# Softmax sums beside the next batch's projections, and loads that wait for the spread of the inverses

## The chip, the cores and the metric

The kernel runs on one core of a Trainium2 chip. The metric is the device time of one execution in microseconds. An engine here is TensorE (PE, matrix products into PSUM), VectorE (DVE), ScalarE (ACT), GpSimd (POOL, which here only starts the loads) or SyncE (SP, which starts stores, on-chip copies and transposes by DMA). Each engine works through its own queue in order and waits on semaphores of the others.

## The reference

Linformer attention is followed by a feed-forward layer with squared ReLU. There are 8 batches, 8 heads, 1024 tokens and 64 channels a head; keys and values are projected from 1024 tokens down to 64.

```
k_proj = einsum('ks,bhsd->bhkd', E, k)           # E, F: 64 x 1024
v_proj = einsum('ks,bhsd->bhkd', F, v)
scores = q @ k_proj^T / sqrt(64)
attn   = exp(scores - max) / (sum(exp(scores - max)) + 1e-9)
x      = attn @ v_proj          # then heads side by side: 8192 x 512
h      = maximum(x @ w_in, 0)   # w_in: 512 x 2048
out    = (h * h) @ w_out        # w_out: 2048 x 512
```

Inputs and output are float32; the kernel multiplies in bf16 and sums in float32 in PSUM.

## The kernel before, in words

**Tiling.** A batch's 1024 tokens form two chunks of 512. The two products of the feed-forward layer are done per chunk by a scheme with seven half-size products in place of eight: operands are first added and subtracted on VectorE (`x_sum`, `w_in_sum`, `s12`, `w_out_sum`), and TensorE then multiplies 128x128 weights by 256 columns. The first product goes by groups of four 128-column blocks of w_in (class `Group`, seven products `p1` to `p7` into four PSUM banks named `ps_bank`, L669); the second goes by `second_spread` into two banks named `ps_second` (L583).

**Steps.** TensorE's order is written out by hand; the other engines' orders come from a scheduler. In the steady part (`both()`) one step is four matmuls of a first product of one chunk, then four of a second product of the chunk before. 28 steps make a chunk and 56 a batch. `at(step, ...)` and `on(step, batch, name)` put a stage of the attention behind a given step. For the loop variable b these steps count from t = 56(b-1)+28; at t+1 the feed-forward work has reached the second chunk of batch b, and the attention of batch b+1 is being finished while that of batch b+2 is begun.

**Attention stages of a batch.** Heads go by pairs, `pr` = 0 to 3.
- `project` (L270, L271): K times E into rows 0 to 63 (`LO`) of the first bank of `ps_att`, V times F into rows 64 to 127 (`HI`) of the second bank; `ps_att` is one buffer of two banks. The other half of each bank is not written. `keep_k` copies K's projection twice into `kp` on VectorE, `keep_v` copies V's into `vp` once on ScalarE and once on VectorE.
- `transpose_k_dma` and `transpose_q_dma` (SP): DMA transposes kp to kT and Q_sb to qT. qT, kT and Q_sb have one buffer each.
- `scores` (L339): two 512-column matmuls into ps_att, then the exponential on ScalarE into `expT`.
- `sums_spread(pr)` (L392): the sums of the exponentials of pairs pr and pr+1, by eight matmuls of 32 columns of ones, into all of ps_att: each pair and each head of it has 32 equal rows of its own. ScalarE takes the logarithm and exp(-x) of 128x1024, which is the inverse (`inv`), and SP copies it by eight DMAs of 32 rows into the two `rs` tiles that the values need (L403). The tag `rs` has three buffers.
- `values(pr)` (L415): four matmuls into ps_att; VectorE multiplies by rs into xT (L419).

The eight quarters of work in sums and values follow this table, whose entries are output rows, bank, head in the pair and input rows:

```
VALUE_QUADS = ((LO, 0, 0, LO), (HI, 1, 1, HI), (HI, 0, 1, LO), (LO, 1, 0, HI))
```

**Loads.** POOL starts them with conversion to bf16: 1 MB of bf16 each for K_sb, V_sb and Q_sb of a batch (L89), one buffer each. In the steady part load_q of batch b+2 is placed at t+11 and waits for the multiplication by rs of pair 1 of batch b+1 (`done`); load_kv of batch b+3 is placed at t+32 and waits for the transpose of K of batch b+2 (`kT_done`). Stores (`put`, L577, 256 KB each, three buffers `o_sb`) stand in SP's queue among the transposes and spreads: four a chunk.

Of the kernel before, what the change touches and what calls it, by code (L numbers as in the profile page):

```python
# [1 line left out]

# [7 lines left out]
P = 128  # L10
F32 = mybir.dt.float32
BF16 = mybir.dt.bfloat16
AF = mybir.ActivationFunctionType
ALU = mybir.AluOpType
PE = mybir.EngineType.PE
LO, HI = slice(0, 64), slice(64, 128)
# [3 lines left out]
def kernel(  # L20
# [11 lines left out]
    nc = tc.nc  # L32

    B, H, S, D = q.shape
# [10 lines left out]
    TCH = S // 2  # L45
# [10 lines left out]
    const_pool = ctx.enter_context(tc.tile_pool(name="const", bufs=1))  # L56
# [4 lines left out]
    soft_pool = ctx.enter_context(tc.tile_pool(name="soft", bufs=3))  # L61
# [5 lines left out]
    turn = {"att": 0, "bank": 0, "step": 1, "pairs": 2}  # L67
# [7 lines left out]
    def att_psum(shape=(P, 2, TCH), dtype=F32):  # L75
        turn["att"] += 1
        return pair_psum(turn["att"] % turn["pairs"], shape, dtype)
# [34 lines left out]
    for g in range(2):  # L112
        h = slice(2 if g == 0 else 4, 4 * g + 4)
# [8 lines left out]
    zeros = const_pool.tile([P, 512], BF16, name="zeros")  # L122
    nc.vector.memset(zeros[:], 0.0)
    ones = const_pool.tile([P, D], BF16, name="ones")
# [7 lines left out]
    for j, (lo, hi) in enumerate(W_IN_PIECES):  # L132
        t = wpool.tile([P, NCB, (hi - lo) * P], BF16, name=f"w_in_{lo}")
# [7 lines left out]
    for j in range(WP):  # L141
        t = wpool.tile([P, fn, DM], BF16, name=f"w_out_{j}")
# [10 lines left out]
    def tt(o, x, op, y):  # L153
        return nc.vector.tensor_tensor(out=o, in0=x, in1=y, op=op)  # L154
# [72 lines left out]
    for h in half:  # L227
        nc.scalar.copy(kp[:, h].rearrange("p h a d -> p (h a d)"), zeros[:])
    kT = const_pool.tile([P, H, 2, KP], BF16, name="kT")
    VALUE_QUADS = ((LO, 0, 0, LO), (HI, 1, 1, HI), (HI, 0, 1, LO), (LO, 1, 0, HI))  # L230

    class Attention:
# [30 lines left out]
            nc.scalar.copy(self.vp[HI], view)  # L263
            nc.vector.tensor_copy(self.vp[LO], view)

        def project(self):
            ps = att_psum()
            for i in range(NI):
                f, l = i == 0, i == NI - 1
                nc.tensor.matmul(ps[LO, 0], lhsT=ET[:, i, :], rhs=self.K[:, :, i, :], start=f, stop=l)  # L270
                nc.tensor.matmul(ps[HI, 1], lhsT=FT[:, i, :], rhs=self.V[:, :, i, :], start=f, stop=l)  # L271
            self.keep_k(ps[LO, 0], slice(0, H))
            self.keep_v(ps[HI, 1])

        def project_k(self, g):
            ps = bank()
            for i in range(NI):
                nc.tensor.matmul(  # L278
                    ps[LO, 0:C // 2], lhsT=ET[:, i, :], rhs=K0[:, half[g], i, :], start=(i == 0), stop=(i == NI - 1)
                )  # L280
            self.keep_k(ps[LO, 0:C // 2], half[g], nc.scalar.copy if g == 0 else None)
# [45 lines left out]
                    )  # L327
            nc.vector.tensor_copy(self.qT[:, 2 * pr:2 * pr + 2], ps[:])

        def transpose_q_dma(self):  # L330
            nc.sync.dma_start_transpose(
                self.qT[:].rearrange("p h n t -> p (h n) t"), self.Q[:].rearrange("p h i d -> p (h i d)")
            )


        def scores_mm(self, ps, pr, n):
# [6 lines left out]
        def sums_mm(self, ps, e):  # L343
            for o, par, a, r in VALUE_QUADS:
                nc.tensor.matmul(ps[o, par], lhsT=ones[r, :], rhs=e[r, a], start=True, stop=True)  # L345

        def values_mm(self, ps, pr, e):
            for o, par, a, r in VALUE_QUADS:
                nc.tensor.matmul(ps[o, par], lhsT=self.vp[r, 2 * pr + a, :], rhs=e[r, a], start=True, stop=True)  # L349
# [17 lines left out]
        def sums(self, pr):  # L367

            ps = att_psum()
            for j in range(2):  # L370
                for o, par, a, r in VALUE_QUADS:
                    c = 32 * (2 * a + j)
# [13 lines left out]
        def sums_spread(self, pr):  # L386

            ps = att_psum()
            for j in range(2):
                for o, par, a, r in VALUE_QUADS:  # L390
                    c = 32 * (2 * a + j)
                    nc.tensor.matmul(  # L392
                        ps[c:c + 32, par], lhsT=ones[r, 0:32], rhs=self.e[pr + j][r, a], start=True, stop=True
                    )
            inv = soft_pool.tile([P, 2, TCH], F32, tag="rs", name="inv")
            nc.scalar.activation(inv[:], ps[:], AF.Ln)
            nc.scalar.activation(inv[:], inv[:], AF.Exp, scale=-1.0)
            for j in range(2):
                rs = soft_pool.tile([P, 2, TCH], F32, tag="rs", name="rs")
                for a in range(2):  # L400
                    have = 32 * (2 * a + j)
                    for to in (64 * a, 64 * a + 32):
                        nc.sync.dma_start(rs[to:to + 32], inv[have:have + 32])  # L403
                self.rs[pr + j] = rs

        def values(self, pr, spare=False):
# [4 lines left out]
            else:  # L411
                ps = att_psum()
                ps_x = [ps[:, par] for par in range(2)]
            for o, par, a, r in VALUE_QUADS:
                nc.tensor.matmul(  # L415
# [32 lines left out]
    class Chunk:  # L448
# [119 lines left out]
        def put(self, a, mh, ps, more=None, part=None, o=None):  # L568
            o = out_pool.tile([P, 2, HM], F32, name="o_sb") if o is None else o
            n = slice(0, 2) if part is None else slice(part, part + 1)  # L570
            ps = ps.rearrange("p (i m) -> p i m", i=2)[:, n]
            if more is None:
                nc.scalar.copy(o[:, n], ps)
            else:
                tt(o[:, n], ps, ALU.add, more.rearrange("p (i m) -> p i m", i=2)[:, n])
            i = 4 * self.c + a + 2 * n.start
            nc.sync.dma_start(  # L577
                out_tokens[self.b][:, i:i + 2 * (n.stop - n.start) - 1:2, mh * HM:(mh + 1) * HM], o[:, n]
            )

# [144 lines left out]
    with tc.manual_schedule(engines={PE}):  # L725
# [33 lines left out]
        def at(step, fn, *args, **kwargs):  # L759
            plan.setdefault(step, []).append(lambda: fn(*args, **kwargs))  # L760
# [13 lines left out]
        atts = {0: att}  # L774
# [90 lines left out]
        def both():  # L865
            f, s = firsts(), seconds()
            for _ in f:
                next(s, None)
                yield

        def on(step, b, name, *args):
            at(step, lambda: getattr(atts[b], name)(*args))
# [5 lines left out]
        for b in range(B - 1):  # L878
            t = 56 * (b - 1) + 28
            if b:  # L880
                on(t + 1, b + 1, "scores", 3)
                on(t + 3, b + 1, "sums_spread", 2)
                on(t + 7, b + 1, "values", 0)
                on(t + 10, b + 1, "values", 1)
                on(t + 20, b + 1, "values", 2)
                on(t + 23, b + 1, "values", 3)
                at(t + 24, lambda b=b: chunk[b + 1, 0].sum_x())
            at(t + 51, lambda b=b: chunk[b + 1, 1].sum_x())
            if b + 2 < B:
                if b:  # L890
                    on(t + 11, b + 2, "load_q", lambda b=b: atts[b + 1].done)
                on(t + (26 if b else 32), b + 2, "transpose_q_dma")
                on(t + (28 if b else 36), b + 2, "project")
                on(t + (30 if b else 37), b + 2, "transpose_k_dma")
                if b + 3 < B:
                    at(t + (32 if b else 37), begin, b + 3)
                    on(t + (32 if b else 37), b + 3, "load_kv", lambda b=b: atts[b + 2].kT_done)
                on(t + (44 if b else 45), b + 2, "scores", 0)
                on(t + (47 if b else 48), b + 2, "scores", 1)
                on(t + (50 if b else 51), b + 2, "sums_spread", 0)  # L900
                on(t + (53 if b else 54), b + 2, "scores", 2)
        steps = both()
        run(steps)
        assert not plan, plan
# [31 lines left out]
```

The softmax here doesn't subtract the row's maximum and nothing guards it: scores larger than these inputs give would overflow.

## Time and profile before

| | |
|---|---|
| median of 3 runs | 474.32 us (473.25 to 474.41) |
| the profiled execution | 473.11 us, span 471.3 us |
| TensorE's granted clock | 1.00 |
| TensorE busy | 464.0 us, 98% of the span |
| VectorE, ScalarE busy | 348.1 us (74%), 297.7 us (63%) |
| one batch of the steady part | 55.4 us: TensorE 55.3, VectorE 43.0, ScalarE 35.6 |
| DMA engines busy in such a batch | 76 to 79%, 158 GB/s |
| rs<-inv | 96 DMAs of 128 KB, 2.3 us to landing |
| qT<-Q_sb, kT<-kp | 6 transposes each, 5.6 and 2.7 us to landing |
| loads of 1 MB | K 10.0, V 14.8, Q 12.1 us to landing |

The page of the profile gives each engine's busy time and the chain of waits that ended last, by engine and by line. Groups of instructions are given by source line, tile and shape, with count, busy time and mean duration. The timeline lists instructions in order of time, the DMA view the transfers with sizes and the time from issue to landing; q0 is the queue of the loads (POOL's), q1 that of SP.

### The profile page before, as it was taken

Reading aid. Unit: us, or ns where it says so; the run is one execution under the profiler, and the core shown is the slowest. Engines: PE = TensorE matmul, PEld = TensorE weight load, DVE = VectorE, ACT = ScalarE, POOL = GpSimd, SP = SyncE. Lnnn points to the kernel's source line nnn. Section 1 sums busy time; section 2 is a strip of 40 time slices with the busy share of each in tenths; the row PEclk is TensorE's granted clock in tenths of the full one; section 3 lists DMA queues with packets and bytes.
Section 4 is the critical chain, followed back from the end, with each engine's and each line's share of the span. In section 5 each row is a group of like instructions: output and inputs, shape, how many; then the busy total and the mean of one; then the engine's idle time right before and its main releaser. Section 6 shows DMA issues by size and latency. Waiting matters only on the chain.

```text
span 471.3 us, 10106 instructions
## 1 busy us (share of the span) xinstructions
PE 464.0 (98%) x4123; PEld 367.6 (78%) x4141; DVE 348.1 (74%) x596; ACT 297.7 (63%) x484; POOL 34.0 (7%) x47
## 2 busy tenths in 40 slices
PE   7999999999999999999999999999999999999997
PEld 4544677888888787887888888888878878888886
DVE  2459985876968779667895679777796778968571
ACT  3488595887467863687556775568736875565641
POOL 7430100100010000100001000100000000000000
PEclk9999999999999999999999999999999999999999
DMA  9999998995869578785978848695692154101012
GB/s 182 201 205 207 160 198 177 178 227 114 176 145 210 142 133 200 128 173 131 174 183 146 169 106 174 154 196 156 108 211 88 31 132 107 68 24 68 24 69 89
DMA packets 85743, 67.90 MB, mean 144 GB/s; under 512 B 34368, under 2 KB 82240, under 8 KB 85696
## 3 DMA queue, kind: packets, MB, share of 16 engines
q0 software_dynamic: 32208, 29.23, 40.7%
q1 hardware_dynamic: 53488, 38.02, 30.2%
q8 instruction: 32, 0.52, 0.4%
q14 instruction: 15, 0.12, 0.1%
HBM read 59.24 MB, written 16.78 MB: 161 GB/s over the span
## 4 chain that ended last, share of the span: by engine, by line
PE 97%; DMA 1%; DVE 1%; ACT 1%; issue 0%; SPq 0%; DVEq 0%
PE ps_bank L669 38%; PE ps_second L583 36%; PE ps_bank L502 6%; PE ps_bank L562 4%; PE ps_att L270 3%; PE ps_att L339 2%; PE ps_att L415 2%; PE ps_second L562 1%; DMA k_f<-in_k_dram 1%; PE ps_att L392 1%; PE ps_bank L314 1%; PE ps_bank L220 1%; PE ps_att L349 1%; PE ps_att L345 1%; PE ps_att L289 0%; PE ps_bank L278 0%
## 5 line engine op out<-in xcount | busy, mean ns | idle before, releaser
L154 DVE TENSOR_TENSOR h<-h 128x1024 bf16<-128x1024 bf16 (+1 forms) x170 | 105.4, 645 | 43.9 <-ACT h L679 38.7
L669 PE MATMUL ps_bank<-x_sum,w_in_sum 128*128 128x256 bf16 x672 | 101.1, 273 | 0.1
L669 PEld LDWEIGHTS <-w_in_sum 128*128 128x128 bf16 x896 | 85.4, 98 | 18.9 <-issue 6.3
L583 PEld LDWEIGHTS <-h 128*128 128x128 bf16 x896 | 87.6, 98 | 10.7
L683 DVE CUSTOM_DVE_ANT_0 h<-ps_bank,u 128x512 bf16<-128x512 f32 x112 | 73.8, 685 | 16.2 <-PE ps_bank L669 12.1
L557 ACT COPY u<-ps_bank 128x512 f32<-128x512 f32 x115 | 68.0, 591 | 24.9 <-PE ps_bank L669 23.7
L694 ACT COPY ps_bank<-ps_bank 128x512 f32<-128x512 f32 x56 | 32.0, 571 | 81.5 <-PE ps_bank L669 81.5
L679 ACT ACTIVATE h<-ps_bank 128x512 bf16<-128x512 f32 x112 | 67.9, 607 | 16.7 <-PE ps_bank L669 15.8
L669 PEld LDWEIGHTS <-w_in 128*128 128x128 bf16 x672 | 64.3, 98 | 14.5 <-issue 5.2
L583 PEld LDWEIGHTS <-s 128*128 128x128 bf16 x672 | 65.7, 98 | 7.6
L669 PE MATMUL ps_bank<-xT,w_in 128*128 128x256 bf16 x448 | 67.3, 273 | 0.3
L583 PE MATMUL ps_second<-w_out_sum,s 128*128 128x256 bf16 x448 | 67.2, 273 | 0.0
L583 PE MATMUL ps_second<-w_out_sum,h 128*128 128x256 bf16 x448 | 67.0, 273 | 0.0
L583 PE MATMUL ps_second<-w_out,h 128*128 128x256 bf16 x448 | 64.7, 272 | 0.0
L419 DVE TENSOR_TENSOR xT<-ps_att,rs 128x512 bf16<-128x512 f32 x48 | 30.9, 685 | 13.7 <-PE ps_att L415 13.7
L353 ACT ACTIVATE expT<-ps_att 128x1024 bf16<-128x1024 f32 x32 | 33.1, 1034 | 5.0 <-PE ps_att L339 3.3
L154 DVE TENSOR_TENSOR o_sb<-ps_second,u 128x512 f32<-128x512 f32 x29 | 19.9, 685 | 19.3 <-PE ps_second L583 13.6
L669 PE MATMUL ps_bank<-x_sum,w_in 128*128 128x256 bf16 x224 | 33.7, 273 | 0.3
L669 PE MATMUL ps_bank<-xT,w_in_sum 128*128 128x256 bf16 x224 | 33.6, 273 | 0.1
L583 PE MATMUL ps_second<-w_out,s 128*128 128x256 bf16 x224 | 33.6, 273 | 0.0
L502 PE MATMUL ps_bank<-xT,w_in 128*128 128x512 bf16 x124 | 28.8, 379 | 0.4 <-issue 0.2
L557 ACT COPY u<-ps_second 128x512 f32<-128x512 f32 x30 | 17.6, 586 | 11.6 <-PE ps_second L583 9.3
(96 smaller groups left out, 458.7 us busy)
## 6 DMA issues: line engine op xcount, KB each, us to landing
out_dram<-o_sb SPq DMA_DIRECT2D x63, 256.0 KB, 2.5
rs<-inv SPq DMA_DIRECT2D x96, 128.0 KB, 2.3
K_sb<-in_k_dram POOLq DMA_DIRECT2D x7, 1024.0 KB, 10.0
V_sb<-in_v_dram POOLq DMA_DIRECT2D x7, 1024.0 KB, 14.8
Q_sb<-in_q_dram POOLq DMA_DIRECT2D x6, 1024.0 KB, 12.1
w_out<-in_moe_w_out_dram POOLq DMA_DIRECT2D x4, 512.0 KB, 15.8
Q_sb<-in_q_dram POOLq DMA_DIRECT2D x4, 256.0 KB, 10.9
V_sb<-in_v_dram POOLq DMA_DIRECT2D x2, 512.0 KB, 11.1
```

The lines of the kernel that those rows point to most:

```text
L154: return nc.vector.tensor_tensor(out=o, in0=x, in1=y, op=op)
L270: nc.tensor.matmul(ps[LO, 0], lhsT=ET[:, i, :], rhs=self.K[:, :, i, :], start=f, stop=l)
L353: self.done = nc.scalar.activation(e[:], ps[:], AF.Exp, scale=SCALE)
L419: self.done = nc.vector.tensor_tensor(out=self.xT[:, pr, :, par], in0=ps_x[par].rearrange("p (c t) -> p c t", c=2), in1=rs[:, par].rearran ...
L502: nc.tensor.matmul(ps[:], lhsT=w_in_blk(cb, fb), rhs=self.xT[:, cb, self.c].rearrange("p a t -> p (a t)"), start=(cb == 0), stop=(cb == NC ...
L557: nc.scalar.copy(u[:], ps)
L562: nc.tensor.matmul(ps[:, i * HM:(i + 1) * HM], lhsT=self.h_form(n, fb)[:, i * P:(i + 1) * P], rhs=w_out_form(n, fb), start=fresh and fb == ...
L583: nc.tensor.matmul(ps[:, i * HM:(i + 1) * HM], lhsT=self.h_form(n, fb)[:, i * P:(i + 1) * P], rhs=w_out_form(n, fb), start=fresh and i == ...
L669: nc.tensor.matmul(ps[:, j * HC:(j + 1) * HC], lhsT=w_in_form(n, cb, 2 * self.g + j), rhs=self.chunk.x_form(n, cb), start=fresh and j == 0 ...
L679: nc.scalar.activation(self.out(kh, a), ps[:], AF.Relu)
L683: nc.vector._custom_dve(TENSOR_ADD_SAT, out=self.out(kh, a), in0=ps[:], in1=more[:], s0=3.0e38, s1=0.0)
L694: nc.scalar.copy(self.chain[:], self.first[:])
```

## The change

In the batches with a further batch to project (b+2 < 8, and b at least 1), the separate `sums_spread(2)` at t+3 is gone. The projection of batch b+2 moves from t+28 to t+9, and with it goes `sums_beside(2)` of batch b+1: the sums of pairs 2 and 3 are written into the two half banks that the projection leaves free. A new constant `pick` has ones in 16 of its 32 columns, which ones depending on the pair, so that both pairs accumulate into the same 32 rows, 16 for each. ScalarE takes the logarithm of each half bank by itself, one before the copies of the projection and one after; one exp(-x) of 128x512 follows, and eight DMAs spread it, each reading 16 rows four times over (64 rows of 2 KB).

Values of pairs 0 and 1 move from t+7 and t+10 to t+4 and t+7. The transpose of K follows at t+10. The load of Q of batch b+2 is placed at t+18 and waits for the last of the spread's DMAs; the loads of K and V of batch b+3 are placed at t+19 and wait for the same. The transpose of Q is at t+28, behind the store put there last. Scores 0, 1 and 2 of batch b+2 move from t+44, t+47, t+53 to t+42, t+45, t+52, and the sums of pairs 0 and 1 from t+50 to t+48. The first batches and the last one keep their order.

```diff
@@ -1,4 +1,4 @@
-from contextlib import ExitStack
+from contextlib import ExitStack, nullcontext
 
 import concourse.bass as bass
 import concourse.tile as tile
@@ -227,6 +227,11 @@
     for h in half:
         nc.scalar.copy(kp[:, h].rearrange("p h a d -> p (h a d)"), zeros[:])
     kT = const_pool.tile([P, H, 2, KP], BF16, name="kT")
+
+    pick = const_pool.tile([P, 2, 32], BF16, name="pick")
+    nc.scalar.copy(pick[:].rearrange("p j k -> p (j k)"), zeros[:, 0:64])
+    for j in range(2):
+        nc.scalar.copy(pick[:, j, 16 * j:16 * j + 16], ones[:, 0:16])
     VALUE_QUADS = ((LO, 0, 0, LO), (HI, 1, 1, HI), (HI, 0, 1, LO), (LO, 1, 0, HI))
 
     class Attention:
@@ -263,14 +268,20 @@
             nc.scalar.copy(self.vp[HI], view)
             nc.vector.tensor_copy(self.vp[LO], view)
 
-        def project(self):
+        def project(self, sums=None):
             ps = att_psum()
             for i in range(NI):
                 f, l = i == 0, i == NI - 1
                 nc.tensor.matmul(ps[LO, 0], lhsT=ET[:, i, :], rhs=self.K[:, :, i, :], start=f, stop=l)
                 nc.tensor.matmul(ps[HI, 1], lhsT=FT[:, i, :], rhs=self.V[:, :, i, :], start=f, stop=l)
+            if sums:
+                sums.sums_beside(2, ps)
+                sums.log(1)
             self.keep_k(ps[LO, 0], slice(0, H))
             self.keep_v(ps[HI, 1])
+            if sums:
+                sums.log(0)
+                sums.spread_beside(2)
 
         def project_k(self, g):
             ps = bank()
@@ -327,10 +338,11 @@
                     )
             nc.vector.tensor_copy(self.qT[:, 2 * pr:2 * pr + 2], ps[:])
 
-        def transpose_q_dma(self):
-            nc.sync.dma_start_transpose(
-                self.qT[:].rearrange("p h n t -> p (h n) t"), self.Q[:].rearrange("p h i d -> p (h i d)")
-            )
+        def transpose_q_dma(self, behind=None):
+            with tc.issue_after(behind.ins) if behind else nullcontext():
+                self.qT_done = nc.sync.dma_start_transpose(
+                    self.qT[:].rearrange("p h n t -> p (h n) t"), self.Q[:].rearrange("p h i d -> p (h i d)")
+                )
 
 
         def scores_mm(self, ps, pr, n):
@@ -403,6 +415,33 @@
                         nc.sync.dma_start(rs[to:to + 32], inv[have:have + 32])
                 self.rs[pr + j] = rs
 
+        def sums_beside(self, pr, ps):
+
+
+            for j in range(2):
+                for o, par, a, r in VALUE_QUADS:
+                    c = HI.start * (1 - par) + 32 * a
+                    nc.tensor.matmul(
+                        ps[c:c + 32, par], lhsT=pick[r, j], rhs=self.e[pr + j][r, a],
+                        start=j == 0, stop=j == 1, skip_group_check=True,
+                    )
+            self.inv = soft_pool.tile([P, 2, TCH], F32, tag="rs", name="inv")
+            self.ps_sums = ps
+
+        def log(self, par):
+            rows = (HI, LO)[par]
+            nc.scalar.activation(self.inv[rows, 0], self.ps_sums[rows, par], AF.Ln)
+
+        def spread_beside(self, pr):
+            inv = self.inv[:, 0]
+            nc.scalar.activation(inv, inv, AF.Exp, scale=-1.0)
+            for j in range(2):
+                rs = soft_pool.tile([P, 2, TCH], F32, tag="rs", name="rs")
+                for o, par, a, r in VALUE_QUADS:
+                    c = HI.start * (1 - par) + 32 * a + 16 * j
+                    self.spread_done = nc.sync.dma_start(rs[o, par], inv[c:c + 16].unsqueeze(1).broadcast_to((16, 4, TCH)))
+                self.rs[pr + j] = rs
+
         def values(self, pr, spare=False):
 
             e, rs = self.e.pop(pr), self.rs.pop(pr)
@@ -574,7 +613,7 @@
             else:
                 tt(o[:, n], ps, ALU.add, more.rearrange("p (i m) -> p i m", i=2)[:, n])
             i = 4 * self.c + a + 2 * n.start
-            nc.sync.dma_start(
+            turn["put"] = nc.sync.dma_start(
                 out_tokens[self.b][:, i:i + 2 * (n.stop - n.start) - 1:2, mh * HM:(mh + 1) * HM], o[:, n]
             )
 
@@ -879,26 +918,34 @@
             t = 56 * (b - 1) + 28
             if b:
                 on(t + 1, b + 1, "scores", 3)
-                on(t + 3, b + 1, "sums_spread", 2)
-                on(t + 7, b + 1, "values", 0)
-                on(t + 10, b + 1, "values", 1)
+                on(t + (4 if b + 2 < B else 7), b + 1, "values", 0)
+                on(t + (7 if b + 2 < B else 10), b + 1, "values", 1)
+                if b + 2 < B:
+                    at(t + 9, lambda b=b: atts[b + 2].project(atts[b + 1]))
+                    on(t + 10, b + 2, "transpose_k_dma")
+                else:
+                    on(t + 3, b + 1, "sums_spread", 2)
                 on(t + 20, b + 1, "values", 2)
                 on(t + 23, b + 1, "values", 3)
                 at(t + 24, lambda b=b: chunk[b + 1, 0].sum_x())
             at(t + 51, lambda b=b: chunk[b + 1, 1].sum_x())
             if b + 2 < B:
                 if b:
-                    on(t + 11, b + 2, "load_q", lambda b=b: atts[b + 1].done)
-                on(t + (26 if b else 32), b + 2, "transpose_q_dma")
-                on(t + (28 if b else 36), b + 2, "project")
-                on(t + (30 if b else 37), b + 2, "transpose_k_dma")
-                if b + 3 < B:
-                    at(t + (32 if b else 37), begin, b + 3)
-                    on(t + (32 if b else 37), b + 3, "load_kv", lambda b=b: atts[b + 2].kT_done)
-                on(t + (44 if b else 45), b + 2, "scores", 0)
-                on(t + (47 if b else 48), b + 2, "scores", 1)
-                on(t + (50 if b else 51), b + 2, "sums_spread", 0)
-                on(t + (53 if b else 54), b + 2, "scores", 2)
+                    on(t + 18, b + 2, "load_q", lambda b=b: atts[b + 1].spread_done)
+                    if b + 3 < B:
+                        at(t + 19, begin, b + 3)
+                        on(t + 19, b + 3, "load_kv", lambda b=b: atts[b + 1].spread_done)
+                    at(t + 28, lambda b=b: atts[b + 2].transpose_q_dma(turn["put"]))
+                else:
+                    on(32 + t, 2, "transpose_q_dma")
+                    on(36 + t, 2, "project")
+                    on(37 + t, 2, "transpose_k_dma")
+                    at(37 + t, begin, 3)
+                    on(37 + t, 3, "load_kv", lambda: atts[2].kT_done)
+                on(t + (42 if b else 45), b + 2, "scores", 0)
+                on(t + (45 if b else 48), b + 2, "scores", 1)
+                on(t + (48 if b else 51), b + 2, "sums_spread", 0)
+                on(t + (52 if b else 54), b + 2, "scores", 2)
         steps = both()
         run(steps)
         assert not plan, plan
```

## The prediction

> **What bounds the kernel now.** I read the shares of the page first, then its chain of waits, then that chain in order of time around the work that is moved, and last the DMA queues, because the change moves transfers too.
>
> ```profile
> PE 464.0 (98%) x4123; PEld 367.6 (78%) x4141; DVE 348.1 (74%) x596; ACT 297.7 (63%) x484; POOL 34.0 (7%) x47
> ...
> PE 97%; DMA 1%; DVE 1%; ACT 1%; issue 0%; SPq 0%; DVEq 0%
> ```
>
> TensorE is the bound: 98% busy and 97% of the chain. Whatever leaves it unchanged can only cost. The next lines are the chain in time round one group of sums (L392), then round the start of a projection (L270).
>
> ```profile
> 206.13 0.44 PE ps_second L583 x4
> 206.57 0.34 PE ps_att L392 x8
> 206.91 0.54 PE ps_bank L669 x4
> ```
> ```profile
> 184.05 0.44 PE ps_second L583 x4
> 184.49 0.33 PE ps_att L270
> ...
> 184.83 0.21 PE ps_att L270
> ```
>
> Four 256-column matmuls take 0.437 us, with nothing between groups: one step is 2 x 0.437 = 0.874 us. A change of tile shape costs about 0.12 us going in (0.33 against 0.21 for the first projection pair) and 0.10 coming back (0.54 against 0.44). The sums cost 0.34 + 0.10 = 0.44 us, one 512-column pass (0.213) plus two changes of shape: all eight matmuls run at once. A projection is 0.33 + 7 x 0.213 = 1.82.
>
> Now the transfers. First SP's queue in time (start, duration), then POOL's, then two DMA windows: 237 to 244 us (stores and query transpose without a load) and 248 to 252 (a store beside a load). Last the queues' packets and MB, from 255 to 257.
>
> ```profile
> 209.46 5.00 SPq L403 DMA_DIRECT2D rs<-inv  x8
> ...
> 237.44 4.10 SPq L331 DMA_TRANSPOSE qT<-Q_sb  x1
> ```
> ```profile
> 225.12 0.87 POOL L89 DMA_DIRECT2D Q_sb<-in_q_dram  x1 [30.74 <-DVE xT L419]
> 248.02 0.87 POOL L89 DMA_DIRECT2D K_sb<-in_k_dram  x1 [22.02 <-DMA kT<-kp]
> 248.88 0.88 POOL L89 DMA_DIRECT2D V_sb<-in_v_dram  x1
> ```
> ```profile
> out_dram<-o_sb SPq DMA_DIRECT2D x3, 256.0 KB, 2.4
> qT<-Q_sb SPq DMA_TRANSPOSE x1, 5.6
> ```
> ```profile
> K_sb<-in_k_dram POOLq DMA_DIRECT2D x1, 1024.0 KB, 10.6
> V_sb<-in_v_dram POOLq DMA_DIRECT2D x1, 1024.0 KB, 14.8
> out_dram<-o_sb SPq DMA_DIRECT2D x1, 256.0 KB, 8.0
> ```
> ```profile
> q0 software_dynamic: 279, 0.28, 83.6%
> q1 hardware_dynamic: 189, 0.19, 34.6%
> ```
>
> Q is issued 23 us before K and V; its transpose starts when it lands (225.1 + 12.3 = 237.4) and ends before K and V start. It never meets a load. A store that does takes 8.0 us in place of 2.4.
>
> **What the Trainium skill says.** "DMA: Bandwidth & Descriptors", section "Queues, rings and completion order": each DMA engine takes its queues in turn, a packet at a time. The trace agrees: in those 2 us the load's queue moved 0.28 MB and SP's 0.19, so SP's transfers get 0.095 MB/us beside a load. "TensorEngine Tiling (Array Packing)", section "Key Properties": a change of tiling mode drains the engine, and different tiles run in parallel; the 0.12 us and the eight sums in 0.34 agree. "PSUM — Partial Sum Buffer", section "PSUM bank collisions raise a hardware error": VectorE and ScalarE may not use one bank and quadrant together, and should be kept apart by semaphores. In this trace the two copies of V's projection on ScalarE (189.34) and VectorE (190.06) follow each other.
>
> **The change part by part.** Write t for the loop's step 56(b-1)+28.
>
> *Sums on TensorE.* Five groups (b = 1 to 5) leave t+3 and join the projection at t+9. Instruction counts stay equal, eight matmuls each. But the two pairs now write the same four 32-column places one after the other (accumulating), so there are two passes: change of shape 0.11 (taken as 0.12 above; this change, 64-column to 32-column tiles, isn't shown) + 2 x 0.213 = 0.54 against 0.44. That is +0.1 a batch, bounded by -0.2 (only one pass longer than nothing) and +0.3 (a pass fails to overlap its weights): +0.5 in all, from -1 to +1.5.
>
> *ScalarE and VectorE.* Two 128x1024 passes (2.08) become three 512-column ones (about 0.58 each, the duration of the V copy). Neither engine is on the path: TensorE's next groups use banks freed a step or more earlier. Cost nothing, covered by the 437 ns groups; up to 0.5 a batch if a bank comes late.
>
> *Values two steps earlier, projection 19 earlier.* ps_att is one buffer. Values 1 at t+7, then two steps = 1.85 us with its change, then the projection. VectorE is busy to about 218.1 with the previous squares, then values 0 (two, 1.29), two ReLU sums (1.2) and values 1 (1.29): done at 221.7, and the projection is due at 221.96. It fits by 0.2; cost nothing, upper bound 0.5 a batch. The projected K must reach kT by t+42, 30 us later: one 2.7 us transpose, hidden. K and V of b+2 were loaded a period before: hidden.
>
> *Loads.* Here the cover goes. Q now waits for the last of eight spread transfers, and K and V for the batch after stand right behind it on POOL. Times from the start of the projection:
>
> - projection and sums 1.82 + 0.54 = 2.4;
> - log, two key copies, V copy, V copy, log, exp, one after the other: 0.58 + 1.3 + 0.58 + 0.69 + 0.58 + 0.58 = 4.3, with one other ScalarE copy between (0.6) and hand-overs (0.3): 7.6;
> - eight spreads: last issued 4.4 after the first (5.00 less one), landing 2.3 later (page, part 6; same bytes, smaller rows: unknown by 1 either way): 14.3;
> - POOL starts 0.6 after its release (kT lands 244.74 + 2.7 = 247.4, K is issued at 248.0): 14.9;
> - Q lands 10.0 later (the median for K, which also starts on idle queues; 12.3 at worst): 24.9;
> - transpose alone 5.6: 30.5.
>
> Due: scores 0, now at t+42. TensorE gets there after 2.4 + 0.1 + 33 steps x 0.874 + two value groups 0.88 = 32.2. So alone there is 1.7 us to spare (before: landed 243.0, due about 255.9, 13 to spare). But K's and V's 2.1 MB start exactly when the transpose does. It moves 1.05 MB (4096 rows of 256 B), 3.7 us at its own 287 GB/s (the trace's rate from 239 to 241); at 0.095 MB/us it takes 11.0, and the loads (2.1 MB at 0.14 = 15 us) outlast it. That is 7.4 more: 37.9, **late by 5.7 us**, and TensorE is in order, so all of it stops. It happens in every batch that has K and V behind Q: b = 1 to 4. At b = 5 there is no further batch to load, and the 1.7 us remain. 4 x 5.7 = 23.
>
> Behind the waiting transpose stand two stores on SP; with three o_sb buffers and the next store at t+49 they delay nobody. Behind Q on POOL stand only K and V, needed 40 us later.
>
> **Sum:** 23 + 0.5 = 23.5 on the profiled execution's 473.1 (span 471.3 and 1.8 around it), 496.6. The median of the runs stands 1.2 above: **498**.
>
> **Bounds of the stall.** The transpose beside a load isn't in this trace. Below: the transpose gets larger turns than a store (its rows are small), +2 in place of +7.4: late by 0.3 or not at all. Above: one 256 B row for one load packet, so that it ends only when K and V are drained (128 load packets an engine at 0.115 us = 15), Q at 12.3: late by 14. I take the measured share of a store, and keep 1 to 10.
>
> **Rivals.**
> 1. *In time* (0.16): transpose and loads hardly disturb each other, or Q lands earlier. For it: 1.7 us to spare alone. Against it: store 2.4 to 8.0. Time 474.3 + 0.5 = 474.8.
> 2. *Hand-overs* (0.05): no late transpose, but ps_att changes hands three times in nine steps, and the 0.2 us doesn't hold: 0.5 to 1 x 5, 477 to 479.
> 3. *Faster* (0.03): the sums ride in the projection's own change of shape and are hidden behind it, which returns the whole 0.44 x 5 = 2.2: 472.1. It decides from a gain of 0.28 a batch; two passes of 0.213 speak against it, and the qT wait has to be absent.
> 4. *The sums don't go away*: so it is; the order of TensorE's instructions keeps all eight, and this is in the sum.
>
> **Chances.** Late transpose 0.76, alone 479 to 514 (1 to 10 us x 4). About 0.3% (1.4 us) is what a measurement of this kernel can tell from no change. Faster 0.03; same 0.16 (rival 1, with a little of the late case below 0.35 us); slower 0.81. The range 475 to 513 leaves out part of rival 1, rival 3 and the top of the late case.
>
> **What would show it.** Right: TensorE idle before L351 (scores), released by the DMA qT<-Q_sb, four times about 6 us; qT's landing about 13 us where 5.6 stood, four times, and 5.6 once; a period of 61 us in place of 55.4. The sums (L424) at 0.54. Wrong: qT landing under 7 us, or no wait at L351; waits at L275 (projection) instead would be rival 2.

## The result, and the profile after

The changed kernel takes 526.84 us (median of six runs, 526.04 to 528.57) against 473.35 for the kernel before beside it (six runs, 472.61 to 474.41): ratio 1.113 [1.111, 1.115]. The change costs 53 us. The forecast was 498 with a range up to 513: the direction and the mechanism hold, the size is off by 28.8 us.

The first lines come from the page of the kernel after: busy time by engine, the granted clock in 40 slices of 13.1 us, and the shares of the chain of waits that ended last.

```profile
PE 474.9 (91%) x4123; PEld 372.5 (71%) x4141; DVE 346.8 (66%) x596; ACT 298.1 (57%) x492; POOL 34.1 (7%) x47
...
PEclk9999999999969999789998799996999999999999
...
PE 59%; DMA 26%; issue 8%; SPq 3%; ACT 2%; DVE 1%; POOLq 0%; DVEq 0%; ACTq 0%
```

TensorE was 97% of the chain and is now 59%; DMA went from 1% to 26%. TensorE does the same 4123 instructions, but its busy time rose by 10.9 us. The clock row says why: it dips in four places, where before it was full throughout.

TensorE's waits (microseconds in total, times, longest), and the table by stage for four periods of a batch (columns: stretch, its length, busy time of PE, PEld, DVE, ACT, POOL, then the granted clock, the busy share of the DMA engines and GB/s; one period is shown):

```profile
PE ps_att L351 <- DMA qT<-Q_sb: 41.9, 5, 10.7
```
```profile
178.90:247.00 68.10, 57.84 (x504) 46.68 (x505) 42.71 (x71) 35.61 (x60) 2.63 (x3) 0.92 0.65 128
```

The four periods that have K and V behind Q take 67.9, 68.1, 68.6 and 67.9 us where 55.4 stood: 50.9 us of the 52.9 by which the span grew (471.3 to 524.2). The fifth wait, at b = 5, is 1.4 us. So the four long ones make 40.5 us, 10.1 each, and about 10 us of the 50.9 are not waiting: in the period shown TensorE is busy for 57.84 us with the work that took 55.3. VectorE and ScalarE do no more than before.

The chain of waits in order of time (start, duration) through the second of these periods shows one wait from its source to its end.

```profile
181.15 0.54 PE ps_att L424 x8
...
192.46 3.00 DMA rs<-inv
...
196.02 10.27 DMA Q_sb<-in_q_dram
...
206.31 15.18 DMA qT<-Q_sb
...
221.52 0.59 PE ps_att L351
...
222.33 1.06 PE ps_bank L708 x4
223.39 0.85 PE ps_second L622 x4
...
228.21 0.44 PE ps_second L622 x4
```

Read it from the top: sums, the last spread of the inverses, the load of Q, its transpose, scores. The transpose, 5.6 us before, takes 15.18. After the wait the four-matmul groups take 0.85 in place of 0.44, up to 227.

What the transpose meets is seen in POOL's issues, in the same period, and then in the transfers between 196 and 222 us (tile, queue, count, KB each, median us to landing) and in the queues' packets, MB and share between 212 and 216.

```profile
196.02 0.88 POOL L89 DMA_DIRECT2D Q_sb<-in_q_dram  x1 [65.50 <-DMA rs<-inv]
196.88 0.89 POOL L89 DMA_DIRECT2D K_sb<-in_k_dram  x1
197.75 0.90 POOL L89 DMA_DIRECT2D V_sb<-in_v_dram  x1
```
```profile
V_sb<-in_v_dram POOLq DMA_DIRECT2D x1, 1024.0 KB, 21.0
...
qT<-Q_sb SPq DMA_TRANSPOSE x1, 15.2
```
```profile
q0 software_dynamic: 611, 0.63, 91.7%
q1 hardware_dynamic: 611, 0.16, 29.6%
```

In four microseconds both queues moved 611 packets. A load's packet holds 1 KB and the transpose's is a row of 256 B, so the loads move 0.158 MB/us and the transpose 0.04, where it has 0.29 alone (0.58 MB from 239 to 241 us of the profile before). At that rate K's and V's 2.1 MB would take 2.1 / 0.158 = 13.3 us. They are done a little sooner, because 0.65 MB of the loads go by in the 3.2 us before the transpose's first rows move: V lands at 218.7, 12.4 us after the transpose was issued. qT lands at 221.5, when its remaining rows have run by themselves.

The sums (L424) take 0.54 us, as forecast, and no wait at the projection (L275) carries any of the loss.

### The profile page after: what moved, and what is told of

Read it like the earlier page. It is cut to its first block, busy times and chain, and to the rows that moved or that the text cites. A ratio compares the mean times of both kernels' runs of the same rounds, so it can differ in the third digit from the quotient of the medians.

```text
span 524.2 us, 10114 instructions
## 1 busy us (share of the span) xinstructions
PE 474.9 (91%) x4123; PEld 372.5 (71%) x4141; DVE 346.8 (66%) x596; ACT 298.1 (57%) x492; POOL 34.1 (7%) x47
## 4 chain that ended last, share of the span: by engine, by line
PE 59%; DMA 26%; issue 8%; SPq 3%; ACT 2%; DVE 1%; POOLq 0%; DVEq 0%; ACTq 0%
PE ps_bank L708 20%; PE ps_second L622 19%; DMA qT<-Q_sb 13%; DMA Q_sb<-in_q_dram 10%; PE ps_bank L541 5%; PE ps_bank L601 3%; SPq L442 3%; DMA rs<-inv 2%; PE ps_att L351 2%; PE ps_att L275 2%; PE ps_second L601 1%; PE ps_att L454 1%; PE ps_bank L220 1%; DMA e_f<-in_E_dram 1%; PE ps_bank L325 1%
## 5 line engine op out<-in xcount | busy, mean ns | idle before, releaser
L708 PE MATMUL ps_bank<-x_sum,w_in_sum 128*128 128x256 bf16 x672 | 102.8, 276 | 0.3
L708 PEld LDWEIGHTS <-w_in_sum 128*128 128x128 bf16 x896 | 87.1, 99 | 18.7 <-issue 4.0
L596 ACT COPY u<-ps_bank 128x512 f32<-128x512 f32 x115 | 67.8, 590 | 24.9 <-PE ps_bank L708 22.7
L722 DVE CUSTOM_DVE_ANT_0 h<-ps_bank,u 128x512 bf16<-128x512 f32 x112 | 73.1, 683 | 10.8 <-PE ps_bank L708 6.9
L708 PEld LDWEIGHTS <-w_in 128*128 128x128 bf16 x672 | 65.5, 100 | 17.1 <-issue 8.6
L622 PEld LDWEIGHTS <-s 128*128 128x128 bf16 x672 | 67.8, 101 | 9.8
L733 ACT COPY ps_bank<-ps_bank 128x512 f32<-128x512 f32 x56 | 32.2, 575 | 70.8 <-PE ps_bank L708 70.8
L622 PE MATMUL ps_second<-w_out_sum,s 128*128 128x256 bf16 x448 | 71.3, 284 | 0.0
L708 PE MATMUL ps_bank<-xT,w_in 128*128 128x256 bf16 x448 | 69.2, 278 | 0.9 <-issue 0.9
L154 DVE TENSOR_TENSOR s<-h 128x1024 bf16<-128x1024 bf16 x32 | 22.0, 691 | 56.8 <-PE ps_second L622 54.9
L351 PE MATMUL ps_att<-qT,kT 128*128 128x512 bf16 (+1 forms) x68 | 17.3, 341 | 42.2 <-DMA qT<-Q_sb 41.9
L351 PEld LDWEIGHTS <-kT 128*128 128x128 bf16 x80 | 7.6, 98 | 45.2 <-issue 43.0
L708 PE MATMUL ps_bank<-x_sum,w_in 128*128 128x256 bf16 x224 | 35.3, 282 | 0.0
## 6 DMA issues: line engine op xcount, KB each, us to landing
K_sb<-in_k_dram POOLq DMA_DIRECT2D x7, 1024.0 KB, 15.2
w_out<-in_moe_w_out_dram POOLq DMA_DIRECT2D x4, 512.0 KB, 15.9
V_sb<-in_v_dram POOLq DMA_DIRECT2D x2, 512.0 KB, 10.9
```

The lines of the kernel that those rows point to most:

```text
L351: nc.tensor.matmul(ps[:, a], lhsT=kT[:, h].rearrange("p g k -> p (g k)"), rhs=self.qT[:, h, n, :], start=True, stop=True)
L596: nc.scalar.copy(u[:], ps)
L622: nc.tensor.matmul(ps[:, i * HM:(i + 1) * HM], lhsT=self.h_form(n, fb)[:, i * P:(i + 1) * P], rhs=w_out_form(n, fb), start=fresh and i == ...
L708: nc.tensor.matmul(ps[:, j * HC:(j + 1) * HC], lhsT=w_in_form(n, cb, 2 * self.g + j), rhs=self.chunk.x_form(n, cb), start=fresh and j == 0 ...
L722: nc.vector._custom_dve(TENSOR_ADD_SAT, out=self.out(kh, a), in0=ps[:], in1=more[:], s0=3.0e38, s1=0.0)
L733: nc.scalar.copy(self.chain[:], self.first[:])
```

## Experiments

The theory after the result: the loss is one chain, spread of the inverses, Q, transpose of Q, and the transpose is slow because K and V are in the queue beside it. Rivals were the sums or the hand-overs of ps_att themselves, the late start of Q alone, a sharing by bytes rather than by packets, and, for the 10 us that are not waiting, TensorE's granted clock against something in the new order of the work.

### K and V behind the transpose

Only the loads of K and V move: they wait for the transpose that they disturbed.

```diff
-                    if b + 3 < B:
-                        at(t + 19, begin, b + 3)
-                        on(t + 19, b + 3, "load_kv", lambda b=b: atts[b + 1].spread_done)
                     at(t + 28, lambda b=b: atts[b + 2].transpose_q_dma(turn["put"]))
+                    if b + 3 < B:
+                        at(t + 29, begin, b + 3)
+                        on(t + 29, b + 3, "load_kv", lambda b=b: atts[b + 2].qT_done)
```

> The changed kernel, but K and V of the batch after wait for the transpose of Q in place of the spread; Q still waits for the spread. Theory A (the transpose takes turns packet for packet with the loads of K and V, and ends only when they are drained): qT lands 6 to 7 us after its issue in place of 14 to 15; what is left is the short wait that the last of the five batches had, 1.4 us, five times; no drop of the clock; 473.35 + 0.5 + 5 x 1.5 = 481 us. Theory B (Q itself is late because of the spread, the loads beside it matter little): waits near 8 us stay, 510 us or more. Theory C (the sums in the projection's banks and the hand-overs of ps_att cost most): no change, 527 us.

Measured: 482.19 us (four runs, 481.43 to 486.53), ratio 1.019 [1.014, 1.024]. The transpose lands in 6.7 to 6.9 us. This is what TensorE still waits for in the profile, which is of the slowest of the four:

```profile
PE ps_att L351 <- DMA qT<-Q_sb: 9.0, 5, 2.9
```

So 44.7 of the 53 us hang on K and V standing beside the transpose. The five waits that remain, 1.2 to 2.9 us, account for the rest: qT is too late even when nothing disturbs its transpose. The clock was expected to stay full. In this profile it did not: behind the wait of 2.2 us it stood at half for 3.4 us.

### Q some 20 steps earlier as well

This kernel is the one above with Q's load moved to the first spread of the batch before (pairs 0 and 1). The new sums stay.

```diff
-                    on(t + 18, b + 2, "load_q", lambda b=b: atts[b + 1].spread_done)
...
+                if b + 3 < B:
+                    on(t + (53 if b else 55), b + 3, "load_q", lambda b=b: atts[b + 2].spread_done)
```
```diff
-                        nc.sync.dma_start(rs[to:to + 32], inv[have:have + 32])
+                        self.spread_done = nc.sync.dma_start(rs[to:to + 32], inv[have:have + 32])
```

> As the kernel with K and V behind the transpose of Q, and Q loaded most of a period earlier: it waits for the first spread of the batch before in place of the second. The sums beside the projection stay. Theory A: no wait on qT at all; what is left is the price of the sums in two passes, 0.1 us x 5: 474 us, no difference that can be measured from 473.35. Theory C: 477 us or more with the loads out of the way. If two passes and a change of shape are cheaper than thought, 472.

Measured: 474.11 us over 20 runs (472.85 to 475.55), ratio 1.000 [0.999, 1.001]. The wait at L351 is gone. One period by stage, in the kernel before and then in this one, and the sums in this one's chain:

```profile
221.50:276.90 55.40, 55.30 (x505) 45.58 (x505) 42.97 (x71) 35.59 (x59) 2.62 (x3) 1.00 0.76 158
```
```profile
221.50:276.90 55.40, 55.20 (x503) 45.55 (x504) 42.72 (x71) 35.39 (x60) 2.62 (x3) 1.00 0.80 157
```
```profile
168.18 0.54 PE ps_att L424 x8
```

The whole loss lies in when the loads start. Sums beside the projection, three hand-overs of ps_att in nine steps and a wider spread cost nothing that can be measured, and they bring nothing: TensorE, which is busy for all of the period, does the same eight matmuls in two passes (0.54) in place of one and a change of shape (0.44). Nothing in these experiments points to a version faster than the kernel before.

### The kernel before, with the late transpose alone

This kernel and its control change the kernel before, so sums and projection stay where they were. The transpose of Q goes from t+26 to behind the store at t+37, so that it meets the loads of K and V, which start at t+32.

```diff
-                on(t + (26 if b else 32), b + 2, "transpose_q_dma")
+                if not b:
+                    on(t + 32, b + 2, "transpose_q_dma")
...
+                if b:
+                    at(t + 37, lambda b=b: atts[b + 2].transpose_q_dma(turn["put"]))
```

> The kernel before, with separate sums and all its loads, but the transpose of Q moved from t+26 to t+37, behind a store, so that it runs beside the loads of K and V (four batches; in the fifth there is no load). Theory A: qT is issued about 195.5 in the time of the profile before, lands when V is drained and some 2 us more, about 210, due at 200.4: four waits of 10 us with a drop of the clock after each of some 2.4 us, and one short wait: about 523 us, nearly the loss of the whole change without any of its sums. Theory C: 475 us.

Measured: 533.85 us, ratio 1.127 [1.123, 1.131], with these waits and landing times (shortest, median, longest):

```profile
PE ps_att L340 <- DMA qT<-Q_sb: 51.7, 5, 13.4
```
```profile
DMA to landing us min/median/max: 5.6/17.2/18.3
```

The collision alone, without any of the change's sums, loses 60 us, more than the whole change (53). That is 11 us more than expected: the four transposes that meet K and V land 17.2 to 18.3 us after their issue, where 14.5 had been reckoned, and the four long waits are 12.3 to 13.4 us and not 10.

The control has the same late transpose, and K and V wait for it at t+38.

```diff
-                    at(t + (32 if b else 37), begin, b + 3)
-                    on(t + (32 if b else 37), b + 3, "load_kv", lambda b=b: atts[b + 2].kT_done)
+                    at(t + 37, begin, b + 3)
+                    on(t + (38 if b else 37), b + 3, "load_kv", lambda b=b: atts[b + 2].qT_done if b else atts[b + 2].kT_done)
```

> Control for the kernel before with its transpose of Q at t+37: the same late transpose, but K and V wait for it, so it runs alone. Theory A: it lands 6.7 us after its issue in place of 17, due some 4 to 5 us after it: five waits of about 2 us, no drop of the clock, 484 us against 533.9. If the late place alone made the loss, it stays near 530.

Measured: 487.67 us, ratio 1.028 [1.026, 1.031]. The landing is back at 5.8 us, and of the lateness 4.6 us remain. Another wait, which wasn't foreseen, is longer: values need ps_att, whose sums ScalarE has not yet inverted. ScalarE's logarithm in turn waits for DMAs. The last line is the first spread (pairs 0 and 1) between 214.5 and 220 us.

```profile
PE ps_att L416 <- ACT inv L397: 7.1, 4, 2.3
PE ps_att L340 <- DMA qT<-Q_sb: 4.6, 5, 1.4
```
```profile
ACT inv L397 <- DMA out_dram<-o_sb: 7.2, 4, 2.3
```
```profile
rs<-inv SPq DMA_DIRECT2D x8, 128.0 KB, 6.3
```

Between these two kernels, which differ in the loads of K and V, lie 46 us. The other 13 are not the price of the late place alone. It accounts for 4.6. In the control K and V run beside the first spread, which lands in 6.3 us where it took 2.3. The logarithm of the next sums needs the buffer that this spread reads (the tag `rs` has three). The profile names a store as the last DMA that ScalarE waited for; the spread's own DMAs landed just ahead of it. So the 7.1 us, and 1.7 more at half clock behind the longest of these waits, most likely go back to K and V as well; no run tries that apart.

### Packets or bytes

Here K's and V's loads of the kernel after are each cut into two halves of four token groups: the same bytes in twice as many packets of 512 B. Q's load stays whole.

```diff
-        dma = load(t[:], tokens(src, b))
+        split = name != "Q_sb" and behind is not None
+        for i in ((slice(0, 4), slice(4, 8)) if split else (slice(0, 8),)):
+            dma = load(t[:, :, i], tokens(src, b, i=i))
```

> The changed kernel, but the loads of K and V of the later batches are cut in two each, so that their packets move 512 bytes in place of 1024 (twice the packets, the same bytes). If the DMA engines take transpose and load in turn packet for packet, both queues count the same number of packets while both run, as they did with 1024-byte packets, and the transpose still ends when the loads are drained: qT lands about 20 us after its issue (twice 128 packets an engine, some 0.085 us a pair, and a start some 4 us late), later than the 15 of the changed kernel, though no byte was added. If they share by bytes, the transpose gets two packets for one of the load and lands at 15 us or sooner.

Measured: 532.68 us (one run). The queues' packets, MB and share between 215 and 219 us, with the transpose that ran there, and TensorE's wait for it:

```profile
q0 software_dynamic: 964, 0.49, 87.6%
q1 hardware_dynamic: 967, 0.25, 46.5%
...
qT<-Q_sb SPq DMA_TRANSPOSE x1, 17.0
```
```profile
PE ps_att L353 <- DMA qT<-Q_sb: 48.2, 5, 12.1
```

Packets are again equal, one for one, while the bytes now stand as two to one in place of four to one. With bytes as the measure the landing would not have moved. It went from 15.2 to 17.0 in this period (14.0 to 15.2 in all four, now 15.9 to 17.3). Beside the transpose the loads now move 0.49 / 4 = 0.123 MB/us in place of 0.158, and V is done 15.5 us after the transpose's issue in place of 12.4. Cutting them does not by itself slow them: in the 3.2 us before the transpose's first rows they move 0.62 MB, the whole loads 0.65. The guess of 20 was too high.

The opposite dose leaves only K beside the transpose, and V waits for it.

```diff
-                        on(t + 19, b + 3, "load_kv", lambda b=b: atts[b + 1].spread_done)
+                        on(t + 19, b + 3, "load_k", lambda b=b: atts[b + 1].spread_done)
                     at(t + 28, lambda b=b: atts[b + 2].transpose_q_dma(turn["put"]))
+                    if b + 3 < B:
+                        on(t + 29, b + 3, "load_v", lambda b=b: atts[b + 2].qT_done)
```

> The changed kernel, but of K and V of the batch after only K follows Q directly; V waits for the transpose of Q. Theory A: half as many load packets stand beside the transpose, 64 an engine, and most of them go before it starts; it lands about 9.5 us after its issue (15 with both, 6.7 with neither), the four waits shrink from 10 to about 5 us and the clock hardly falls: 497 us. Theory B (Q late because of the spread, the loads beside it don't matter): 525 us.

Measured: 499.87 us, ratio 1.054 [1.052, 1.057].

```profile
DMA to landing us min/median/max: 6.7/8.6/9.6
```
```profile
PE ps_att L357 <- DMA qT<-Q_sb: 18.0, 5, 4.9
```

With no load beside it the transpose takes 6.7 us, with 1 MB 8.2 to 9.6, with 2 MB 14.0 to 15.2: its landing follows what the loads still have to move. The waits came out as expected, 3.9 to 4.9 us, but the clock did not: it fell behind all four of them, with 14.2 us of work at half speed, 7.1 us lost.

### The clock

In the kernel after, TensorE's busy share, its granted clock, the DMA share and GB/s by microsecond round the wait that ends at 221.5:

```profile
211.00:212.00 1.00, 0.54 (x5) 1.00 1.23 198
...
216.00:217.00 1.00, 0.00 (x0) 0.81 1.20 194
217.00:218.00 1.00, 0.00 (x0) 0.50 1.35 182
...
223.00:224.00 1.00, 1.00 (x6) 0.50 0.00 0
...
226.00:227.00 1.00, 1.00 (x7) 0.56 0.00 0
227.00:228.00 1.00, 1.00 (x10) 1.00 0.00 0
```

TensorE stops at 211.5, its clock falls to half at about 216.6, work resumes at 221.5, and the clock returns at about 226.9 (a mean of 0.56 in that microsecond is 0.88 us at half). That is 5.4 us of work at half speed, or 2.7 us lost; over the four waits such stretches come to some 10 us lost, which is the 10 us that are not waiting. "TensorE: Matmul & The Clock Gate", section "Part 1: The HAM clock gate (the "warmup" mystery)", names these two states and a window of 3413 ns that runs by itself, in which activity is counted. The records agree: half speed lasts 10.2 us each time, three such windows, and the four falls stand 68.27 us apart, twenty of them.

To separate this from the new order of the work, matmuls on zeros into the ps_att that scores will overwrite fill the wait in b = 1 to 4: 45 of 512 columns, 9.6 us at 0.213 each.

```diff
             ps = att_psum()
+            for _ in range(filler):
+                nc.tensor.matmul(ps[:, 0], lhsT=zeros[:, 0:P], rhs=zeros[:], start=True, stop=True)
```

> The changed kernel, but TensorE multiplies zeros 45 times (512 columns, 0.213 us each: 9.6 us) into ps_att ahead of scores 0 of the four batches with the long wait. Clock theory (after a wait of some 10 us TensorE is granted half its clock for about 4 us, which costs 2.4 us a batch): the waits shrink to under 1 us, the scores start when they did, the clock stays at 1.00, and 4 x 2.4 is saved: 517 us. Rival (the clock falls because of the transfers or for another reason than the wait): 527 us, clock 0.96.

Measured: 517.24 us, ratio 1.091 [1.089, 1.093]; the clock row of its page:

```profile
PEclk9999999999999999999999999999999999999999
```

The data still arrive as late (qT 14.3 to 15.9 us after its issue; up to 1.2 us of waiting are left behind the zeros), and the kernel gains 526.84 - 517.24 = 9.6 us: the clock's share.

With 28 of them a wait of 4 to 5 us is left over.

> As the changed kernel with 45 multiplications of zeros ahead of scores 0, but 28 (6.0 us), so that some 4.5 us of waiting are left in each of the four batches. In the changed kernel's trace the clock falls 4.9 us after TensorE's last matmul. If that is a delay that counts from the last matmul, the clock stays at 1.00 here and the time is that of 45, 517 us. If any wait of that kind costs clock in proportion to its length, it falls between, about 521 us.

Measured: 527.0 us (523.75 to 530.22), ratio 1.112 [1.106, 1.118], above both of the expected times (517 and 521). The same view of this kernel by microsecond:

```profile
217.00:218.00 1.00, 0.15 (x1) 1.00 1.35 133
...
222.00:223.00 1.00, 1.00 (x8) 0.68 0.40 122
223.00:224.00 1.00, 1.00 (x7) 0.50 0.00 0
...
226.00:227.00 1.00, 1.00 (x9) 1.00 0.00 0
```

TensorE stops at 217.15 and resumes at 221.65 with its clock still full. The clock falls at about 222.4, when TensorE has been at work again for 0.7 us, and stays at half for one window of 3.4 us, all of it in work: 1.7 us lost. The four waits of this kernel, 4.5 to 5.1 us, lose 7.1 us in that way. That is most of the 10 us over 517; the other 3 us weren't traced, and lie within the 6.5 us over which its runs spread. Shortening a long wait to 4 or 5 us does not bring the clock back.

Which waits cost the clock can be read from all the traces together. In each of them every change of the clock lies on one grid of 3.413 us. From 100 to 440 us, in all ten traces, the clock fell at the end of each of the 22 windows of this grid at full clock in which TensorE stood idle for 2.1 us or more, and at the end of none with 1.9 us or less; nothing lies between. Idle time isn't the whole rule: in the first 100 us one fall, at 7.9 us of the kernel before with the late transpose, follows a window with 1.6 us. In the steady part a wait counts by how it falls on the grid. The kernel with K and V behind the transpose shows both cases: its wait of 2.87 us lies across a boundary (at 146.75) and costs nothing, its wait of 2.15 us lies in one window and is followed by a fall. The lines are TensorE's busy time and clock in the two windows of the first wait, the one window of the second, and the one after it.

```profile
143.34:146.75 3.41, 1.76 (x17) 1.00 1.22 218
146.75:150.16 3.41, 2.13 (x18) 1.00 0.64 186
259.39:262.80 3.41, 1.25 (x11) 1.00 1.13 253
262.80:266.22 3.42, 3.20 (x16) 0.50 0.50 102
```

## Why the prediction was wrong, and where it was right

**Right.** The bound (TensorE, and then a late transpose of Q), its place (L351), the four long waits and the one batch without K and V behind Q. In the period shown the projection starts at 179.31. The first spread is issued 7.6 us after that (forecast 7.6), and TensorE reaches scores 0 at 32.2 (forecast 32.2). The sums at 0.54 and the hand-overs at nothing hold too; the kernel with the early Q shows both at once.

**Wrong: three terms of the sum.** Times after the start of the projection, in the period shown:

| step | forecast | measured | added here |
|---|---|---|---|
| first spread issued | 7.6 | 7.6 | 0 |
| last spread landed | 14.3 | 16.1 | +1.8 |
| Q issued | 14.9 | 16.7 | 0 |
| Q landed | 24.9 | 27.0 | +0.3 |
| qT landed | 37.9 | 42.2 | +2.2 |
| scores 0 due | 32.2 | 32.2 | 0 |
| late by | 5.7 | 10.0 | +4.3 |

1. *The transpose beside loads*, "at 0.095 MB/us it takes 11.0": the rate was that of a store beside a load, turned into bytes. What the transpose and the loads share is packets, and a transpose's are 256 B where a store's were 1 KB (0.19 MB in 189 packets). Its rate there is 0.04 MB/us. The right mechanism stood in the upper bound, "one 256 B row for one load packet", and the count of 611 to 611 is it. The forecast took the middle, although the view that it quoted, 279 packets against 189 and 0.28 MB against 0.19, was a count of packets of one size: it could not tell bytes from packets, and it wasn't one for one either (taken as packets, 189 rows in 2 us would have made 0.024 MB/us, too slow). This cost 2.2 us here, and 14.0 to 15.2 us to landing in the four batches against 13.0.

2. *The spread*, "eight spreads: last issued 4.4 after the first ... same bytes, smaller rows: unknown by 1 either way": eight issues of 64 rows take 6.1 us (5.0 for 32 rows), the last starts 5.5 after the first, and it lands in 3.0 us (2.3). That is +1.8, outside its own bound. Why such a DMA takes longer to issue wasn't tried. Q, taken at 10.0, took 11.5, 10.3, 10.3 and 10.8.

3. *The clock* had no term. A wait of 10 us was priced as 10 us of lost time; it costs some 2.5 more (9.6 over four waits).

Summed: the four waits 40.5 in place of 23 (+17.5), the clock (+9.6), the fifth wait (+1.4) where 1.7 us to spare was expected. Together 28.5, against the 28.8 by which the median missed. One more term of the forecast is off: with no load beside it the transpose takes 6.7 to 6.9 us in this kernel and not 5.6, even the first one (6.8, at 79.9 us), which comes ahead of the steps that the change moves; no run tells why.

**The range** let the stall be 1 to 10 us a batch, although the forecast's own upper bound was 14; four times 10.1, and the clock on top, lie beyond its end. Rivals 1 and 2 are excluded by the waits, rival 3 by the kernel with the early Q.

**What stays open.** The transpose's first rows appear 3 to 4 us after its issue when loads are queued (SP's queue moved nothing from 206.3 to 209.5 us, and 107 packets in the next 1.5); no run tells why. Between 1.9 and 2.1 us of idle time in a window of the clock's grid nothing was measured.

## What to carry to other kernels

Before a load is moved, list what will share the DMA queues with it and with whatever waits for it, and price the sharing in packets where the trace counts them equal: here a transfer of 4096 small rows, beside loads of 2048 large packets, ended only after the loads had. Put a large load behind the small transfer that the bound engine needs next; here this one edge was worth 45 of 53 us. And when a stall of TensorE is several microseconds long, add the stretch at half clock behind it to its price: 1.5 to 3 us here.

## What the runs showed of the hardware

- A DMA transpose of 256 B rows and loads share one for one by packets: 611 to 611 with 1 KB load packets, 964 to 967 with 512 B. The transpose falls from 0.29 to 0.04 MB/us, and cutting the loads' packets in half brings its landing later, not earlier (15.2 to 17.0 us).
- The granted clock changes on a grid of 3.41 us. From 100 to 440 us it fell at the end of every window of it, at full clock, in which TensorE was idle for 2.1 us or more, and of none with 1.9 us or less. Its falls came 2.1 to 5.3 us after the last matmul, also when TensorE had resumed by then, and half speed lasted 3.4, 6.8, 10.2 or 13.7 us, one to four windows.
- Matmuls on zeros hold the clock: 45 of 512 columns in each wait kept it at 1.00 and returned 9.6 us of 526.84.
